# A list of steps for the first three slots, and weight loads in other places and packets, in a kernel of attention and soft mixture of experts

## The chip, the cores and the metric

The kernel runs on one core of one Trainium2 chip. The time is device microseconds of one execution; the figure for a kernel is the median of several runs. A profiled execution has its own time and, inside it, a span from the first to the last instruction; all positions below (such as "at 20.98") are microseconds from the start of that span. Engines are named as in the profile: PE is the matrix engine (PEld its weight loads), DVE the vector engine, ACT the scalar engine, POOL the general engine that also issues most DMAs, SP the engine that issues the rest.

## The reference

Attention first, with a softmax that has one extra term in its denominator, over 8 batches of 12 heads, 448 tokens and 64 features:

```python
scores = (q @ k.T) / sqrt(64)
m = max(scores); e = exp(scores - m)
attn = e / (sum(e) + exp(-m) + 1e-9)
x = (attn @ v)              # to [3584, 768], heads side by side
```

Then a soft mixture of 8 experts with 4 slots each. Logits `x @ phi` give two softmaxes: `d` over all 3584 rows, which mixes rows into 32 slots, and `c` over the 32 slots, which mixes the slots' results back.

```python
slot_input = d.T @ x                                   # [8, 4, 768]
slot_out[e] = relu(slot_input[e] @ w1[e]) @ w2[e]      # w1 768x1024, w2 1024x768
out = c @ slot_out                                     # [3584, 768]
```

q, k, v are 11 MB each in float32, w1 and w2 25 MB each; every one of them is turned to bfloat16 by the DMA that loads it. The row maximum must be known before the exponential is taken.

## The kernel before, in words

**Pairs and slots.** Two heads of one batch make a pair: 48 pairs, numbered n. The first part of the kernel is a loop over slots s = 0 to 48, each with two halves y = 0, 1; a slot handles one pair's attention and, beside it, earlier work of later pairs and later work of earlier ones. The engines' orders are written out by hand: an engine runs its instructions in the order in which the program issues them, so the place of a step in the loop is its place in every engine's queue.

**The steps of a pair n**, with the lines that the profile shows for them:

- `T(n)`: 28 transpositions of q and k pieces on PE (L255) into one bank, one copy out (L262 on ACT, for the first nine pairs always).
- `A(n, i)`, i in the order 0, 3, 1, 2: scores for the row maxima, two matmuls (L293, or L303 for i = 3) into banks of `psA`, which has three, and a maximum by DVE of each bank (L297, L306). `As(c)` takes the next c entries of the list `runs` of all (n, i). From slot 3 on most of them are fused into `Bk` (L284, L286).
- `W1(g)`: on POOL, the maxima of a group of pairs, negated and set out (L313, L317). `W2(g)`: four matmuls turn them (L335, L336). `W3(g)`: copy and exponentials on ACT (L341 to L347). Groups are pair 0; pairs 1 and 2; then three pairs each.
- `Bk(n, i)`: scores transposed (L366 or L395), the maximum taken off by a second matmul (L369 or L398), exponential on ACT (L371 or L401). Between the two matmuls it can issue one `A`.
- `AV(n, i, qs)`: products with V (L435), into the one bank of `psV`; `N1(n)` copies them out (L448, on ACT), `N2(n)` divides (two small DVE steps, then POOL, L468 to L479), `PX(n)` transposes the result (L500, copy L506).
- `V(g)`: POOL copies of v into its padded form (L407 to L410); `load(g, nm)` the DMAs of q, k or v for three pairs (L175, L179, L180, POOL).

After pair group b of six, the pieces `P(b)` of the logits and slot sums are hung into later slots (`post`).

**Weights.** `halves` lists w1 of the 8 experts (0 to 7), then w2 of the 8 experts (8 to 15), each a tile of 768 x 1024 bfloat16. Tiles 0 to 10 have memory of their own and are loaded in two transfers each during the loop: `half_at` says after which slot. w1 is read with rows p, p+128, ... on partition p, so that a packet is one row, 2,048 bytes in bfloat16; w2 with 8 neighbouring rows on a partition, so that half a tile is one packet of 6,144 bytes for each partition. Tiles 11 to 15 go, row by row (40 rows of 128 x 768), where the attention's own buffers lie, as these come free: `rows_at`. Some of the rows, `stage_at`, are first copied to a scratch tensor in HBM in bfloat16 (L145, POOL) and fetched from there late (L153, SP).

**End.** After slot 48: `hidden(g)` (w1 products of four experts, L848), `turn(g)` (transposes the hidden layer, L860; its columns are taken with a step of 8, to fit the 8 neighbouring rows of w2 on a partition), `slots(g)` (w2 products, L867), then the output (L904 to L926).

**The first slots.** Ahead of the loop the program issues, written out, T and A steps of pairs 0 to 2, the first group's `W1` to `W3`, and four DMAs; slots 0 to 2 then go through the loop with conditions of their own (`early`, `hs == 1`, `hs < 5`).

Of the kernel before, what the change touches and what calls it, by code (L numbers as in the profile page):

```python
# [9 lines left out]
BF16 = mybir.dt.bfloat16  # L10
# [21 lines left out]
def kernel(  # L32
# [10 lines left out]
    nc = tc.nc  # L43
    B, H, S, D = q.shape
    DD = H * D
# [63 lines left out]

    def load_part(i, z0, z1):  # L110
        kind, e = halves[i]
        src = (moe_w1 if kind == "w1" else moe_w2)[e].rearrange("(j p) f -> p j f" if kind == "w1" else "(p j) f -> p j f", p=128)
        gdma(out=w_sb[(kind, e)][:, z0:z1, :], in_=src[:, z0:z1, :])  # L113

    def load_half(i, z, t=None):
# [25 lines left out]
    def stage_rows(r0, r1):  # L141
        i, z = divmod(r0, FK)
        assert r1 <= (i + 1) * FK
        t = dram.tile([128, r1 - r0, DD], BF16, name=f"stage{r0}")
        gdma(out=t, in_=moe_w2[11 + i - E].rearrange("(p j) f -> p j f", p=128)[:, z:z + r1 - r0, :])  # L145
        staged[r0, r1] = t

# [8 lines left out]
    with ExitStack() as at:  # L156
# [83 lines left out]
        def T(n):  # L240
            g, pl = divmod(n, NP)
            first = n < NP * NP
            ps = psB.tile([128, 2, S], BF16, tag="b", name="ps_t")

            k0 = [psB.tile([128, 2, S], BF16, tag="b", name="ps_k") for _ in range(2)] if n == 0 else None
            for a in range(2):
                src = nat["qk"[a], g]
                order = [(tok, hl) for tok in range(7) for hl in range(2)]
                if a and n == 0:
                    order.sort(key=lambda z: kcol(z[1], z[0]))  # L250
                for tok, hl in order:
# [3 lines left out]
                    nc.tensor.transpose(o, src[r, pl, tok * D:(tok + 1) * D], ident[r, r])  # L255
# [428 lines left out]
        def As(c):  # L684
            for _ in range(min(c, len(runs))):
                A(*runs.pop(0))
# [3 lines left out]
        ps = psV.tile([128, 512], F32, tag="v", name="ps_idle")  # L690
        for _ in range(22):
            nc.tensor.matmul(ps[:, 0:64], wm[0][:, 0, :], wm[0][:, 0, 0:64], start=True, stop=True)
        T(0)
        As(2)
        T(1)
        As(2)
        W1(0)
        V(0)
        load(1, "v")
        ones_in(vp[1], nc.gpsimd)  # L700
        As(1)
        T(2)
        W2(0)
        W3(0)
        As(1)
        for nm in "qk":
            load(2, nm)
        for z in range(2):
            load_half(0, z, w_tile(0))

        half_at = {s: i + 1 for i, s in enumerate((1, 4, 7, 10, 13, 19, 22, 28, 31, 34))}


        rows_at = {77: 3, 83: 7, 85: 12, 89: 17, 91: 20, 92: 24, 93: 26, 95: 27}
        rows = 0
        stage_at = {18: (16, 24), 37: (27, 32), 38: (32, 36), 40: (36, 40)}
        wait_loads = []
        waits = [r for z in stage_at.values() for r in range(*z)]  # L720
        for s in range(NPAIR + 1):
            for y in range(2):
                hs = 2 * s + y
                early = int(hs < 4)
                mix = s >= 3 and len(runs) > 1 and runs[0][1] == 1 - y
                if mix:
                    Bk(s, 2 * y, mix=True)
                    Bk(s, 2 * y + 1, y, mix=True)
                else:
                    As(1)  # L730
                if mix:
                    pass
                elif s < NPAIR:
                    Bk(s, 2 * y)
                    As(early)
# [5 lines left out]
                if hs == 1:  # L741
                    W1(1)
                if hs < 5:
                    T(hs + 3)
                if y == 0:
                    if 0 <= s - 1:
                        for i in (2, 3):
                            AV(s - 1, i, range(3))
                else:
                    if 2 <= s < NPAIR - 6:  # L750
# [23 lines left out]
                As(early)  # L774
                if hs == 1:
                    W2(1)
                    W3(1)
                if y == 0 and s and s + 1 in firsts:
                    W1(mg(s + 1))
                if y == 0 and wait_loads:  # L780
                    f, z = wait_loads.pop()
                    f(z)
                if y == 0 and s % 3 == 2 and (s + 1) // 3 < NG:
                    if s == 2:
                        load(2, "v")
                    if s == NPAIR - 4:
                        V(NG - 1)
                    if s - 1 in half_at:
                        load_half(half_at[s - 1], 0, w_tile(half_at[s - 1]))
                if y == 0 and hs in rows_at:  # L790
                    load_rows(rows, rows_at[hs])
                    rows = rows_at[hs]
            def slot_loads(s):
                g = (s + 10) // 3
                if s == 1 or (s and s % 3 == 2):
                    if g < NG:
                        load(g, "q")
                        load(g, "k")
                g = (s + 9) // 3
                if s % 3 == 0 and g - 2 < NG - 1:  # L800
                    V(g - 2)
                    if s and g - 1 < NG:
                        load(g - 1, "v")
                if s - 1 in half_at:
                    load_half(half_at[s - 1], 1)
                if s in stage_at:
                    stage_rows(*stage_at[s])
# [47 lines left out]
        def turn(g):  # L855
            n = FK // (1 + g)
            for k0 in range(0, FK, n):
                ps = psA.tile([128, n, 128], BF16, tag="a", name="ps_ht")
                for kt in range(k0, k0 + n):
                    nc.tensor.transpose(ps[:, kt - k0, :], h[g].rearrange("p (d k) -> p k d", k=FK)[:, kt, :], ident)  # L860
# [156 lines left out]
```

## Time and profile before

| what | us |
|---|---|
| median of 3 runs (lowest, highest) | 300.39 (299.71, 301.83) |
| profiled execution | 300.82 |
| its span | 299.0 |
| last copy of attention products, L448 on DVE | 248.6 |
| busy PE, DVE, ACT, POOL in the span | 272.7, 249.7, 250.7, 193.3 |
| mean granted PE clock | 0.957 |

The 1.8 us between span and time lie around the instructions. A busy share is a mean over very different parts: a start of 34 us, in which the engines fill one after another; some 210 us in which PE, DVE and ACT are all nearly full; and the end, experts and output, in which they take turns. A "chain" line follows the work back from the last instruction; a "waits" line says which engine's line waited for whom. PE counts as busy while a matmul sits in it, even if that is slowed by another.

### The profile page before, as it was taken

To read this page: it belongs to the slowest core of one execution; us is meant where nothing else is said; L and a number is where in the kernel's file an instruction comes from. 1 tells how busy PE (TensorE), PEld (TensorE's weight loads), DVE (VectorE), ACT (ScalarE), POOL (GpSimd) and SP (SyncE) were. 2 spreads that over 40 slices of the span, in tenths; PEclk is the share of its full clock that TensorE was granted. 3 is DMA by queue.
4 is the path that set the end of the run, shared out by engine and by line. 5 is a ranking of instruction groups with operands and counts; after the bars stand their busy time and mean duration, and the time that the engine had idled before them with its cause. 6 is when DMAs were issued, how large, how long until landed. Compare 5 with 4: busy or idle time off the path is not lost.

```text
span 299.0 us, 12393 instructions
## 1 busy us (share of the span) xinstructions
PE 272.7 (91%) x5174; PEld 162.8 (54%) x5174; DVE 249.7 (83%) x581; ACT 250.7 (84%) x559; POOL 193.3 (65%) x389
## 2 busy tenths in 40 slices
PE   5989999999999999899999999999999999996810
PEld 4434556565666566557566666666565556652100
DVE  5889799999999999899999999998999675437930
ACT  4567999999899989898999899989999987337820
POOL 8791997879778959886969697978775633000000
PEclk9999999999999999999999999999999999997555
DMA  7999799999999978999998999999999689808997
GB/s 137 142 145 208 115 207 207 209 207 207 193 189 171 197 101 120 193 189 207 210 153 113 151 192 162 194 178 207 181 196 197 120 177 266 329 4 323 380 448 322
DMA packets 40103, 58.67 MB, mean 196 GB/s; under 512 B 2752, under 2 KB 30912, under 8 KB 39744
## 3 DMA queue, kind: packets, MB, share of 16 engines
q0 software_dynamic: 35072, 42.29, 85.8%
q1 hardware_dynamic: 4976, 15.60, 13.3%
q8 instruction: 40, 0.66, 0.8%
q14 instruction: 15, 0.12, 0.1%
HBM read 89.16 MB, written 15.14 MB: 349 GB/s over the span
## 4 chain that ended last, share of the span: by engine, by line
PE 73%; ACT 11%; DVE 5%; issue 3%; POOL 2%; DMA 1%; DVEq 0%; POOLq 0%; ACTq 0%
PE ps_av L435 16%; PE ps_a L284 11%; PE ps_b L366 8%; PE ps_b L369 7%; PE ps_t L255 6%; PE ps_b L395 5%; PE ps_b L398 3%; PE ps_x L500 3%; PE ps_o L910 3%; ACT W L401 2%; ACT W L262 2%; DVE mx L297 2%; ACT W L506 2%; PE ps_s L622 2%; PE ps_h L848 2%
## 5 line engine op out<-in xcount | busy, mean ns | idle before, releaser
L286 DVE TENSOR_REDUCE mx<-ps_a 128x1 f32<-128x448 f32 x250 | 137.4, 613 | 5.2 <-PE ps_a L284 4.4
L371 ACT ACTIVATE W<-ps_b 128x448 bf16<-128x448 f32 x250 | 120.4, 575 | 0.0
L284 PE MATMUL ps_a<-W 64*128 64x448 bf16 x250 | 80.8, 352 | 0.1
L366 PE MATMUL ps_b<-W 64*128 64x448 bf16 x250 | 70.2, 352 | 1.3
L369 PE MATMUL ps_b<-mT,sel 64*128 64x448 bf16 x250 | 66.3, 350 | 0.1
L435 PEld LDWEIGHTS <-W 128*128 128x128 bf16 (+1 forms) x1536 | 50.3, 100 | 27.4 <-issue 23.6
L435 PE MATMUL ps_av<-W 128*128 128x65 bf16 (+1 forms) x1536 | 64.5, 196 | 0.3 <-issue 0.3
L468 POOL TENSOR_TENSOR W<-ubuf,rec 128x384 bf16<-128x384 f32 x44 | 36.3, 826 | 38.6 <-ACT W L506 19.2
L401 ACT ACTIVATE W<-ps_b 128x448 bf16<-128x448 f32 x86 | 45.5, 572 | 4.2 <-PE ps_b L398 4.2
L255 PEld LDWEIGHTS <-W 64*64 64x64 bf16 x1344 | 29.2, 112 | 13.0 <-issue 4.7
L506 ACT CAST W<-ps_x 128x512 bf16<-128x512 f32 x47 | 28.6, 607 | 6.4 <-PE ps_x L500 6.1
L255 PE MATMUL ps_t<-ident,W 64*64 64x64 bf16 x1330 | 30.4, 195 | 2.6 <-ACT W L214 1.3
L306 DVE TENSOR_REDUCE mx<-ps_a 128x1 f32<-128x448 f32 x48 | 29.5, 615 | 1.5 <-PE ps_a L303 1.5
L284 PEld LDWEIGHTS <-W 64*128 64x128 bf16 x250 | 23.3, 94 | 9.8
L369 PEld LDWEIGHTS <-sel 64*128 64x128 bf16 x250 | 19.5, 94 | 14.8 <-issue 6.0
L395 PE MATMUL ps_b<-W 64*64 64x448 bf16 (+1 forms) x134 | 26.9, 374 | 0.3
L113 POOL DMA_DIRECT2D W<-in_moe_w_dram x30 | 20.9, 698 | 7.7 <-PE ps_b L398 7.7
L262 ACT COPY W<-ps_t 128x896 bf16<-128x896 bf16 x21 | 19.6, 933 | 7.2 <-PE ps_t L255 7.2
L448 ACT COPY ubuf<-ps_av 128x455 f32<-128x455 f32 x44 | 25.1, 571 | 0.3
L398 PE MATMUL ps_b<-mT,sel 64*64 64x448 bf16 (+1 forms) x134 | 24.9, 354 | 0.2
L297 DVE TENSOR_REDUCE mx<-ps_a 128x1 f32<-128x448 f32 x38 | 20.9, 616 | 2.1 <-PE ps_a L293 2.1
L479 POOL TENSOR_TENSOR W<-ubuf,rec 128x128 bf16<-128x128 f32 x44 | 17.6, 400 | 3.7
(156 smaller groups left out, 447.2 us busy)
## 6 DMA issues: line engine op xcount, KB each, us to landing
W<-in_moe_w_dram POOLq DMA_DIRECT2D x24, 768.0 KB, 10.1
W<-in_v_dram POOLq DMA_DIRECT2D x32, 192.0 KB, 6.4
out_dram<-W SPq DMA_DIRECT2D x2, 2688.0 KB, 10.0
W<-in_q_dram POOLq DMA_DIRECT2D x15, 336.0 KB, 6.2
W<-in_k_dram POOLq DMA_DIRECT2D x15, 336.0 KB, 7.2
out_dram<-W SPq DMA_DIRECT2D x6, 384.0 KB, 3.0
out_dram<-W SPq DMA_DIRECT2D x3, 768.0 KB, 4.9
W<-stage SPq DMA_DIRECT2D x3, 576.0 KB, 5.6
```

The lines of the kernel that those rows point to most:

```text
L255: nc.tensor.transpose(o, src[r, pl, tok * D:(tok + 1) * D], ident[r, r])
L284: nc.tensor.matmul(ps[:, 0:S], t[r, 0, i * 128:(i + 1) * 128], t[r, 1, :], start=True, stop=True)
L286: nc.vector.reduce_max(m[:, c:c + 1], ps[:, 0:S], axis=AX.X)
L366: nc.tensor.matmul(pss[hl][:, 0:S], t[rs[hl], 1, cols], t[rs[hl], 0, :], start=True, stop=False)
L369: nc.tensor.matmul(pss[hl][:, 0:S], sel[rs[hl], 2 * pl + hl:2 * pl + hl + 1].to_broadcast([64, 128]), mT[mg(n)][rs[hl], :], start=False, s ...
L371: nc.scalar.activation(e[:, hl, :], pss[hl][:, 0:S], AF.Exp, scale=scale)
L395: nc.tensor.matmul(outs[hl], t[rs[hl], 1, cols], t[rs[hl], 0, :], start=True, stop=False)
L398: nc.tensor.matmul(outs[hl], sel[rs[hl], 2 * pl + hl:2 * pl + hl + 1].to_broadcast([64, m]), mT[mg(n)][rs[hl], :], start=False, stop=True)
L401: nc.scalar.activation(e, p[:, 0:S], AF.Exp, scale=scale)
L435: nc.tensor.matmul(o, eT[n, i, hl][:, qc], vp[g % 2][:, 2 * pl + hl, i, 0:W65], start=(i == 0 and u == 0 and hl == 0) or (u == 3 and i == ...
L468: eng.tensor_mul(x[:, 0:3, c:c + 128].rearrange("p i (h d) -> p i h d", h=2), u[:, 0:6, 0:D].rearrange("p (i h) d -> p i h d", h=2), rec[: ...
L506: nc.scalar.copy(xT(b, pb), pss[0])
```

## The change

1. The w2 tiles of experts 0 to 3 are read as w1 is, row p, p+128, ... on partition p: packets of 1,536 bytes instead of 4,608 or 6,144. `turn(0)` accordingly takes 128 neighbouring columns instead of every eighth.
2. The scratch tensor gets rows that are 32 elements longer than their content, so that neighbouring rows no longer join: the staging and the fetches go in packets of 1,536 bytes.
3. `half_at` is every third slot from 4 to 31 instead of (1, 4, 7, 10, 13, 19, 22, 28, 31, 34). Rows 16 to 24 are staged in slots 35 and 36 instead of 18, rows 27 to 40 half a slot to two and a half slots later than before, each staging in two transfers. The second transfer of a tile is issued in the first half of the next slot, not at the end of its own.
4. Slots 0 to 2 and what stood ahead of them are one list of words, run in order. The steps and their number are the same, and so is the state at slot 3 (26 `A` steps taken, T up to pair 8); the tile 1 of w1 is no longer loaded in it. Between steps, the places differ: T(2) stands ahead of A(1,0) (before: between A(1,0) and A(1,3)); A(3,1) and A(3,2) ahead of `W2(1)` (before: behind it); products with V are cut into single steps i, with `A` or `Bk` between them.

```diff
-        src = (moe_w1 if kind == "w1" else moe_w2)[e].rearrange("(j p) f -> p j f" if kind == "w1" else "(p j) f -> p j f", p=128)
+        src = (moe_w1 if kind == "w1" else moe_w2)[e].rearrange(
+            "(j p) f -> p j f" if kind == "w1" or e < E // 2 else "(p j) f -> p j f", p=128)
...
-        t = dram.tile([128, r1 - r0, DD], BF16, name=f"stage{r0}")
+        t = dram.tile([128, r1 - r0, DD + 32], BF16, name=f"stage{r0}")[:, :, 0:DD]
...
-        T(0)
-        As(2)
-        T(1)
-        As(2)
-        W1(0)
-        V(0)
-        load(1, "v")
-        ones_in(vp[1], nc.gpsimd)
-        As(1)
-        T(2)
-        W2(0)
-        W3(0)
-        As(1)
-        for nm in "qk":
-            load(2, nm)
-        for z in range(2):
-            load_half(0, z, w_tile(0))
-        half_at = {s: i + 1 for i, s in enumerate((1, 4, 7, 10, 13, 19, 22, 28, 31, 34))}
+        half_at = {s: i + 1 for i, s in enumerate(range(4, 32, 3))}
...
-        stage_at = {18: (16, 24), 37: (27, 32), 38: (32, 36), 40: (36, 40)}
+        stage_at = {34: [(16, 20), (20, 24)], 37: [(27, 29), (29, 32)], 40: [(32, 36), (36, 40)]}
...
+        ramp = ("T0 A A T1 A A W0 T2 A G0 A X0 J0 A B0.0 A B0.1 A A T3 A B0.2 A A T4 C0.3 V0.0 W1 A V0.1 V0.2 A X1 T5 "
+                "A B1.0 A K0 V0.3 H0 C1.1 N0 B1.2 A T6 C1.3 V1.0 V1.1 A B2.0 M0 K1 A T7 B2.1 A V1.2 V1.3 W2 T8 H1 A "
+                "N1 B2.2 Y2 V2.0 X2 C2.3 Z0 V2.1 M1 K2 ")
+        for word in ramp.split():
...
+        for s in range(3, NPAIR + 1):
...
+                if y == 0 and s - 1 in stage_at:
+                    stage_rows(*stage_at[s - 1][0])
+                if y == 0 and s - 2 in half_at:
+                    load_half(half_at[s - 2], 1)
+                if y == 0 and s - 2 in stage_at:
+                    stage_rows(*stage_at[s - 2][1])
...
-                    nc.tensor.transpose(ps[:, kt - k0, :], h[g].rearrange("p (d k) -> p k d", k=FK)[:, kt, :], ident)
+                    nc.tensor.transpose(ps[:, kt - k0, :], h[g].rearrange("p (d k) -> p k d" if g else "p (k d) -> p k d", k=FK)[:, kt, :],
+                                    ident)
```

In the list, B and C are `Bk` (C with an `A` between its two matmuls), V one step i of `AV` for the first three blocks of rows and H the last block for all i, W is `W1`, X is `W2` with `W3`, N and M are `N1` and `N2`, Z is `PX(0)`. G is `V(0)`, the load of v for group 1 and its padding; J loads q and k of group 2 and tile 0 of w1; K(s) is what the end of slot s issued (K0: `V(1)`; K1: q and k of group 3; K2: of group 4); Y loads v of group 2.

More of the change, by code (lines that the diff above doesn't have):

```diff
@@ L716, with slot_loads @@
         rows_at = {77: 3, 83: 7, 85: 12, 89: 17, 91: 20, 92: 24, 93: 26, 95: 27}
         rows = 0
-        stage_at = {18: (16, 24), 37: (27, 32), 38: (32, 36), 40: (36, 40)}
+        stage_at = {34: [(16, 20), (20, 24)], 37: [(27, 29), (29, 32)], 40: [(32, 36), (36, 40)]}
         wait_loads = []
-        waits = [r for z in stage_at.values() for r in range(*z)]
-        for s in range(NPAIR + 1):
+        waits = [r for z in stage_at.values() for y in z for r in range(*y)]
+        def slot_loads(s):
+            g = (s + 10) // 3
+            if s == 1 or (s and s % 3 == 2):
+                if g < NG:
+                    load(g, "q")
+                    load(g, "k")
+            g = (s + 9) // 3
+            if s % 3 == 0 and g - 2 < NG - 1:
+                V(g - 2)
+                if s and g - 1 < NG:
+                    load(g - 1, "v")
@@ new lines @@
+        ramp = ("T0 A A T1 A A W0 T2 A G0 A X0 J0 A B0.0 A B0.1 A A T3 A B0.2 A A T4 C0.3 V0.0 W1 A V0.1 V0.2 A X1 T5 "
+                "A B1.0 A K0 V0.3 H0 C1.1 N0 B1.2 A T6 C1.3 V1.0 V1.1 A B2.0 M0 K1 A T7 B2.1 A V1.2 V1.3 W2 T8 H1 A "
+                "N1 B2.2 Y2 V2.0 X2 C2.3 Z0 V2.1 M1 K2 ")
+        for word in ramp.split():
+            op, arg = word[0], [int(z) for z in word[1:].split(".") if z]
+            if op == "T":
+                T(*arg)
+            elif op == "A":
+                As(1)
+            elif op in "BC":
+                Bk(*arg, int(op == "C"))
+            elif op == "W":
+                W1(*arg)
+            elif op == "X":
+                W2(*arg)
+                W3(*arg)
+            elif op == "V":
+                AV(*arg, range(3))
+            elif op == "H":
+                for i in range(4):
+                    AV(arg[0], i, [3])
+            elif op == "N":
+                N1(*arg)
+            elif op == "M":
+                N2(*arg)
+            elif op == "G":
+                V(0)
+                load(1, "v")
+                ones_in(vp[1], nc.gpsimd)
+            elif op == "J":
+                for nm in "qk":
+                    load(2, nm)
+                for z in range(2):
+                    load_half(0, z, w_tile(0))
+            elif op == "Y":
+                load(2, "v")
+                if 1 in half_at:
+                    load_half(half_at[1], 0, w_tile(half_at[1]))
+            elif op == "Z":
+                PX(0)
+            elif op == "K":
+                slot_loads(*arg)
@@ L722 @@
+        for s in range(3, NPAIR + 1):
             for y in range(2):
                 hs = 2 * s + y
-                early = int(hs < 4)
-                mix = s >= 3 and len(runs) > 1 and runs[0][1] == 1 - y
+                mix = len(runs) > 1 and runs[0][1] == 1 - y
                 if mix:
@@ L734 @@
                     Bk(s, 2 * y)
-                    As(early)
                     side = int(y == 1 and len(runs) > 0 and runs[0][1] == 3)
@@ L740 @@
                     As(1)
[L741 to L744, printed above, removed]
                 if y == 0:
-                    if 0 <= s - 1:
-                        for i in (2, 3):
-                            AV(s - 1, i, range(3))
+                    for i in (2, 3):
+                        AV(s - 1, i, range(3))
                 else:
-                    if 2 <= s < NPAIR - 6:
+                    if s < NPAIR - 6:
                         T(s + 6)
@@ L773 @@
                         N2(s - 1)
[L774 to L777, printed above, removed]
                 if y == 0 and s and s + 1 in firsts:
@@ L783 @@
                 if y == 0 and s % 3 == 2 and (s + 1) // 3 < NG:
-                    if s == 2:
-                        load(2, "v")
                     if s == NPAIR - 4:
@@ L792 @@
                     rows = rows_at[hs]
[L793 to L807, printed above, removed]
             if s > 2 and s + 2 in firsts:
```

## The prediction

> **What bounds the kernel now.** First the page's busy times and its 40 slices (7.5 us each).
>
> ```profile
> PE 272.7 (91%) x5174; PEld 162.8 (54%) x5174; DVE 249.7 (83%) x581; ACT 250.7 (84%) x559; POOL 193.3 (65%) x389
> PE   5989999999999999899999999999999999996810
> DVE  5889799999999999899999999998999675437930
> ACT  4567999999899989898999899989999987337820
> ```
>
> From slice 5 to 31 PE, DVE and ACT are all at 8 or 9: a stretch with nothing to gain from moving a step, except where a slice dips. The first four slices are lower, ACT's most. One slice inside dips on all three rows (slice 17, from 120 us). So I asked for the engines' sums in the start and just behind it (columns: length, then busy PE, PEld, DVE, ACT, POOL, granted clock, DMA share, GB/s).
>
> ```profile
> 5.70:34.10 28.40, 25.93 (x415) 13.31 (x414) 25.08 (x49) 18.85 (x37) 18.79 (x44) 1.00 1.00 147
> 34.10:41.90 7.80, 7.42 (x124) 3.94 (x124) 6.49 (x13) 7.80 (x20) 7.47 (x13) 1.00 1.25 205
> ```
>
> From the first maximum to slot 3 DVE works 25.08 of 28.40 us: it is the engine nearest to full, and 3.32 us are idle. Behind it ACT is busy 7.80 of 7.80: the start leaves a backlog there, and the chain of work runs on ACT from 33.16 to 40.5. A gain in the start counts only if ACT, too, gets its work earlier. The places where DVE idled (the bracket: us idle, and who ended it):
>
> ```profile
> 11.97 0.62 DVE L306 TENSOR_REDUCE mx<-ps_a 128x1 f32<-128x448 f32 x1 [0.92 <-PE ps_a L303]
> ...
> 20.98 3.28 DVE L297 TENSOR_REDUCE mx<-ps_a 128x1 f32<-128x448 f32 x6 [0.67 <-PE ps_a L293]
> 24.70 0.62 DVE L306 TENSOR_REDUCE mx<-ps_a 128x1 f32<-128x448 f32 x1 [0.43 <-PE ps_a L303]
> ...
> 31.92 1.16 DVE L297 TENSOR_REDUCE mx<-ps_a 128x1 f32<-128x448 f32 x2 [0.48 <-PE ps_a L293]
> ```
>
> Each time PE was on something else (T, W2, V products) and the three banks of `psA` had run dry. Two smaller gaps, 0.36 at 7.78 and 0.18 at 19.70, and the delays between instructions make the rest.
>
> The dip in slice 17 is on PE's own timeline:
>
> ```profile
> 124.37 0.44 PE L255 MATMUL ps_t<-ident,W 64*64 64x64 bf16 x17
> 125.69 0.35 PE L255 MATMUL ps_t<-ident,W 64*64 64x64 bf16 x11 [0.87 <-issue]
> ...
> 214.05 0.28 PE L435 MATMUL ps_av<-W 128*128 128x65 bf16 x4 [0.35 <-issue]
> ```
>
> PE stops between the 17th and 18th of 28 transpositions, with no semaphore to wait for ("issue"), and again inside four V products at 213.7. These are the only two such stops of over 0.2 us in the full stretch. What they share is in the DMA view of the first one's stretch, 119 to 127:
>
> ```profile
> DMA packets 299, 1.72 MB, mean 215 GB/s; under 512 B 16, under 2 KB 249, under 8 KB 249
> q0 software_dynamic: 297, 1.69, 109.3%
> q8 instruction: 1, 0.02, 0.8%
> ```
>
> 50 packets are over 8 KB: 48 of them are the staging of rows 16 to 24, 1,536 KB, so 32 KB each; the trace's packet records give them 2.43 to 3.43 us apiece. The q8 packet is one of 40 in the run, 16 KB each, with PE's instructions. On average one comes every 250 PE instructions; this one, at 123.46, comes 410 behind the last. I read it as a refill that sat behind 32 KB packets until PE ran out. At 211.36 the next such packet takes 1.39 us (others 0.9 to 1.0) among packets of 7,680 bytes (587 ns), and PE stops at 213.71. No refill beside packets of 2,048 (173 ns) or 6,144 bytes (474 ns) is followed by a stop.
>
> **The change part by part.**
>
> *The list of steps.* All 26 A keep their order and number, so DVE has the same 25 us of work; only gaps can go. T(2), 0.96 us of PE, now stands ahead of A(1,0): A(1,0) starts later, A(1,3) right behind it; of 0.92 I count 0.45 gone. At 20.98 PE waited for `W1(1)`, which POOL reached at 19.76 behind five us of DMAs and memsets; that POOL order is unchanged, but A(3,1) and A(3,2) now stand ahead of `W2(1)`, four maxima of 0.55 (3.28 for six), so DVE works through: 0.67 and 0.18 gone. At 24.70, T(5) and 20 V products (0.72) lay between two A; now A(4,0) parts them: 0.43 gone. At 31.92, twelve V products (0.47), T(8) (0.56) and H1 lie between A(5,2) and A(6,0): stays. Sum 0.45 + 0.67 + 0.18 + 0.43 = 1.73.
>
> ACT the same way: from `W3(1)` at 20.69 to slot 3's first exponential at 35.47 it has 14 exponentials, 4 copies of T, 2 of N1, and 1.7 of the rest. Back to back (29.36 to 35.47) an exponential takes 0.43, a T copy 0.79, an N1 copy 0.43: 6.0 + 3.2 + 0.9 + 1.7 = 11.8. Against 14.8 that is 3.0 at most. Putting the new order down with these durations, three A banks, and DVE without the gaps above, slot 3's exponential starts near 33.7: 1.7 gained. Both agree on **1.7**.
>
> What is late next: q and k of group 3. Here k landed at 37.30 and T(9) starts to load at 37.82. Their issue (31.02) stands behind `N2(0)` on POOL, and `N2(0)`'s two DVE steps now stand behind one maximum more (0.55), which eats most of DVE's lead there; so k lands some 0.5 earlier, T(9) would like 1.7 earlier, and PE waits about 0.7. ACT is the full engine there and has three exponentials queued; I count 0.2. **Net 1.5.** Bounds: 0 (ACT's backlog takes the gaps) and 3.0.
>
> *Packets and places.* No packet over 8 KB from POOL is left in the full stretch, and none of 7,680 bytes. The two stops are 0.87 + 0.35 = 1.22. By the N1 copies, which come once a slot, six slots take 29.03 (70.50 to 99.53) and 28.98 (158.73 to 187.71), but 29.96 (99.53 to 129.49) and 29.51 (187.71 to 217.22): 0.95 + 0.50 = 1.45. I take **1.4**; bounds 0 (the stops recur elsewhere) and 1.7.
>
> What it costs: a 1,536-byte packet takes 134 ns, four of them 536 against 474 for one of 6,144: 13% more DMA time for w2 of four experts and for the staging. A group of three slots then needs 1,024 x 134 + 768 x 88 + 768 x 60 ns over 16 engines = 15.7 us of packet time for w2, q, k and v, against 15.4 with a w1 tile, in 14.5 us; packets overlap, the share reached 1.23 with w1, and no T waited. So nothing is added: the cover is 3.5 slots between a load of q and k and its T. If that went, a T would wait. POOL issues with three pieces for each partition take 0.78 against 0.58; some 0.2 to 0.3 x 10 on an engine that is idle for a third. Bound: 1.0 lost.
>
> *turn(0).* Its loads of the matrix engine step by 8 elements; the others of 128 x 128 do not:
>
> ```profile
> L860 PEld LDWEIGHTS <-ubuf x8: 142/148/166, 260.5 to 261.0; 128*128 128x128 bf16 x8
> ```
>
> Against a median of 97 for L500's. Eight loads by 50 ns are 0.4, partly under the transpositions: I take **0.1**, bounds 0 and 0.4. By the Trainium skill, "TensorE: Matmul & The Clock Gate", section "Weight-path perf modes", the fast load holds for any column step up to 1,024 elements, so the step would cost nothing and this term be 0; the row, 148 against 97, speaks against it.
>
> *Sum.* 1.5 + 1.4 + 0.1 = 3.0. The profiled execution took 300.82 (span 299.0 and 1.8 around it), so 297.8; it lies 0.4 above the median of the runs shown, so the forecast for that is **297.4**.
>
> **Rivals.** *(a) Only the packets count:* ACT's full stretch behind slot 3 and the wait of T(9) take the start's gain. For it: 7.80 of 7.80, and 0.5 us of slack at T(9). Against: ACT idled 2.3 us between 21.4 and 29.4. 300.4 - 1.5 = 298.9. *(b) The change doesn't do what it says:* the stops come from the refill's own timing, not from long packets, and show up elsewhere; the start gains a little: 300.0. For it: only two cases. Against: some 25 refills beside packets of 512 to 6,144 bytes without a stop. *(c) Slower: late w2.* The stagings of rows 32 to 40 move from 211.6 and 222.4 to about 222 and 227, where rows 3 to 12 are loaded too. Eight rows of 128 packets of 134 ns over 16 engines are 8.6 us of DMA time, in a stretch whose share was 1.08 (220 to 230) and 0.65 (230 to 240). The last fetch landed at 262.03, and the w2 products of experts 4 to 7 that need it start near 266: the margin is 4 us. If all 8.6 us are late, PE waits 4.4: 297.4 + 4.4 = 301.8. It decides from a delay of 4 us on; beyond +1% it leads only from 10 us on. Against: 3.5 us of free DMA time from 230 to 240. The Trainium skill, "DMA: Bandwidth & Descriptors", section "Rules for kernel authors", wants transfers coalesced, 1 MiB and more, which speaks for (c); no row here shows a PE wait from short packets. *(d) More:* DVE's gaps all go and ACT follows (3.0), and 1.7 for the packets: 295.6.
>
> **How the numbers follow.** A measurement of this kernel tells about 1% (3 us) from no change; the forecast lies on that bound. Chances: forecast 0.55 (half of it beyond the bound), (a) 0.17, (b) 0.08, (c) 0.12 (half of it with a delay of over 10 us), (d) 0.08. Faster: 0.28 + 0.08, and 0.07 from (a), should the packets alone bring twice what I count: 0.43. Slower: 0.06. Same: the rest, 0.51. The range, 295.4 to 300.8, leaves out the outer ends of (c) and (d).
>
> **What would show it.** Right: no PE stop by "issue" over 0.2 us between 34 and 245; q8 packets evenly spaced; DVE idle under 1.8 us up to slot 3; slot 3's first exponential near 33.7; T(9) with a short wait for q or k. Wrong: a PE wait for DMA behind 255; slot 3 no earlier; a stop by "issue" at some other place; ACT as full behind slot 3 and its first exponential at 35.

## The result, and the profile after

| | before | after |
|---|---|---|
| median (lowest, highest), 20 runs each | 300.45 (299.29, 307.34) | 298.47 (297.57, 300.78) |
| ratio of after to before, 95% | | 0.993 (0.991 to 0.9949) |
| profiled execution, its span | 300.82, 299.0 | 300.78, 299.0 |

The change gains 0.7%, 1.98 us by the medians; 297.4 was forecast for the median and 295.4 to 300.8 as the range. Before's 307.34 is one of the few runs that are slow as a whole, and the ratios leave such runs out. The profiled execution of after is the longest of its 20 runs, so its trace shows losses that the typical run has less of. A second profile of the same kernel (e3, below) took 298.90.

First the page's busy times and slices of the profile after:

```profile
PE 271.4 (91%) x5174; PEld 162.5 (54%) x5174; DVE 249.7 (84%) x581; ACT 249.8 (84%) x559; POOL 195.9 (66%) x391
PE   5999899999999999999899999999999999996820
DVE  5899799999999989999889999998999675537930
ACT  3569999999899989998989899989999987337820
```

The work is the same, but the dips have moved: PE's slice 17 (from 120 us) is 9 now, and slice 20 (from 142 us) is 8. The sums of the start and of what follows it (length, then busy PE, PEld, DVE, ACT, POOL, granted clock, DMA share, GB/s):

```profile
5.70:34.10 28.40, 26.09 (x424) 13.65 (x423) 25.50 (x50) 20.04 (x42) 19.61 (x45) 1.00 1.04 157
34.10:41.90 7.80, 7.66 (x160) 4.54 (x158) 7.31 (x16) 7.80 (x18) 6.51 (x13) 1.00 1.22 181
```

ACT did 1.19 us more in the same 28.40 (it had 18.85), and still is busy 7.80 of 7.80 behind it. The best marker for the rest of this text is the copy `N1` of each slot's attention products (`ubuf` from `ps_av`, L449 now), once a slot at fixed places of the work. Each entry is its start after minus its start before:

| copy of slot | 5 | 10 | 15 | 20 | 25 | 30 | 45 | whole execution |
|---|---|---|---|---|---|---|---|---|
| after | -1.62 | -1.61 | -1.61 | -0.96 | -1.63 | +0.10 | +0.12 | -0.04 |
| after once more (e3) | -1.61 | -1.61 | -1.61 | -0.92 | -2.15 | -2.20 | -1.94 | -1.92 |

The start gains 1.6 us, and keeps it up to slot 16. Then both executions lose 0.65 to 0.69 at one place. Between slots 20 and 25 before itself loses 1.2, around its stop at 124.8, and e3 is 2.15 ahead; the profiled execution of after loses 2.3 between slots 20 and 30. The waits that answer to this, on the timeline of after (start, length, engine, line, tiles, and in the bracket the idle time ahead and who ended it), DVE first:

```profile
10.52 1.16 DVE L298 TENSOR_REDUCE mx<-ps_a 128x1 f32<-128x448 f32 x2 [0.40 <-PE ps_a L294]
...
30.22 1.16 DVE L298 TENSOR_REDUCE mx<-ps_a 128x1 f32<-128x448 f32 x2 [0.48 <-PE ps_a L294]
32.75 0.62 DVE L307 TENSOR_REDUCE mx<-ps_a 128x1 f32<-128x448 f32 x1 [1.37 <-PE ps_a L304]
```

Of the gaps shown of before, 0.92 has become 0.40, those of 0.67 and 0.43 are gone, that of 0.48 stands as it was. A new one of 1.37 is ahead of the list's last maximum. PE's timeline of after:

```profile
31.11 0.34 PE L436 MATMUL ps_av<-W 128*128 128x65 bf16 x6 [0.62 <-ACT ubuf L449]
32.01 0.34 PE L336 MATMUL ps_m<-ident,W 128*128 128x128 bf16 x3 [0.55 <-POOL W L314]
104.06 0.34 PE L336 MATMUL ps_m<-ident,W 128*128 128x128 bf16 x3 [0.59 <-POOL W L314]
143.26 0.38 PE L256 MATMUL ps_t<-ident,W 64*64 64x64 bf16 x12 [0.60 <-issue]
150.01 0.52 PE L436 MATMUL ps_av<-W 128*128 128x65 bf16 x12 [1.10 <-issue]
164.05 0.35 PE L256 MATMUL ps_t<-ident,W 64*64 64x64 bf16 x11 [0.34 <-issue]
201.96 0.22 PE L436 MATMUL ps_av<-W 128*64 128x65 bf16 x2 [0.48 <-issue]
```

The first two are what PE waited for inside DVE's 1.37: V2.0 waits for N1(1), and `W2(2)` waits for `W1(2)` on POOL. The third is the loss of 0.6 near slot 17, again a wait for POOL. The last four, 2.52 us, are stops of the kind that the shorter packets were forecast to end: they name no semaphore, and there is no packet over 2,048 bytes from POOL near them.

### The profile page after: what moved, and what is told of

Same layout as the page of the kernel before. It is cut to its first block, busy times and chain, and to the rows that moved or that the text cites. A ratio compares the mean times of both kernels' runs of the same rounds, so it can differ in the third digit from the quotient of the medians.

```text
span 299.0 us, 12398 instructions
## 1 busy us (share of the span) xinstructions
PE 271.4 (91%) x5174; PEld 162.5 (54%) x5174; DVE 249.7 (84%) x581; ACT 249.8 (84%) x559; POOL 195.9 (66%) x391
## 4 chain that ended last, share of the span: by engine, by line
PE 68%; ACT 10%; DVE 6%; POOL 6%; issue 4%; DMA 2%; DVEq 0%; POOLq 0%; ACTq 0%
PE ps_av L436 15%; PE ps_a L285 10%; PE ps_b L367 7%; PE ps_b L370 7%; PE ps_t L256 5%; PE ps_b L396 5%; PE ps_x L501 3%; PE ps_b L399 3%; ACT W L402 2%; PE ps_o L925 2%; DVE mx L298 2%; PE ps_s L623 2%; PE ps_h L862 2%; PE ps_so L882 2%; ACT W L263 2%
## 5 line engine op out<-in xcount | busy, mean ns | idle before, releaser
L114 POOL DMA_DIRECT2D W<-in_moe_w_dram x30 | 22.6, 755 | 7.9 <-PE ps_b L399 7.8
L449 ACT COPY ubuf<-ps_av 128x455 f32<-128x455 f32 x44 | 25.1, 571 | 0.8 <-POOL W L408 0.6
```

## The experiments

All compare with the kernel before on the same chip: e1 to e4 on one (before's median there was 301.4), e7 to e10 on a second (300.81), e5, e6, e12 and e13 on a third (301.64). Across these sets ratios are to be compared, not times. "Over lowest" is how far a kernel's median lies above its own lowest run. "Profiled" is the time of the execution that the profile shows: a profile of a kernel's fastest run says little of the losses of its usual one.

| run | list of steps | places | packets | median (runs) | ratio to before (95%) | over lowest | profiled |
|---|---|---|---|---|---|---|---|
| e1 | new | old | long | 299.34 (12) | 0.9925 (0.9893 to 0.9956) | 1.6 | 297.78 |
| e2 | old | new | short | 300.07 (12) | 0.9975 (0.9948 to 1.0001) | 0.7 | 300.76 |
| e3 (= after) | new | new | short | 298.66 (12) | 0.9914 (0.988 to 0.9948) | 0.6 | 298.90 |
| e4 | new | fewer loads | short | 298.05 (6) | 0.9899 (0.9864 to 0.9935) | 0.2 | 299.42 |
| e5 | old | new | long | 301.78 (12) | 1.0019 (0.9994 to 1.0044) | 2.0 | 304.73 |
| e6 | old | old | short | 300.47 (12) | 0.9967 (0.9942 to 0.9993) | 1.2 | 300.29 |
| e7 | new | new | long, w1 too | 298.97 (12) | 0.9951 (0.9926 to 0.9976) | 1.0 | 297.98 |
| e8 | reordered | new | short | 297.73 (6) | 0.9902 (0.9871 to 0.9932) | 0.6 | 297.88 |
| e9 | new | moved | short | 298.03 (12) | 0.9912 (0.9883 to 0.9942) | 0.6 | 298.24 |
| e10 | reordered | moved | short | 297.67 (6) | 0.9903 (0.9871 to 0.9934) | 0.6 | 297.97 |
| e12 | reordered | moved | long | 297.32 (6) | 0.9885 (0.9843 to 0.9927) | 0.8 | 297.61 |
| e13 (= e10) | reordered | moved | short | 297.27 (6) | 0.9876 (0.9844 to 0.9907) | 0.6 | 297.77 |

"Short" has turn(0)'s new reading with it. The kernel before lay 1.9, 1.6 and 2.4 over its lowest run in the three sets. The profile of e5 was taken in an execution 2.9 us over its median and is not read for stops.

### e1, e2, e3: the two halves of the change apart

e1 is after with these lines of before:

```diff
-            "(j p) f -> p j f" if kind == "w1" or e < E // 2 else "(p j) f -> p j f", p=128)
+            "(j p) f -> p j f" if kind == "w1" else "(p j) f -> p j f", p=128)
-        t = dram.tile([128, r1 - r0, DD + 32], BF16, name=f"stage{r0}")[:, :, 0:DD]
+        t = dram.tile([128, r1 - r0, DD], BF16, name=f"stage{r0}")
-        half_at = {s: i + 1 for i, s in enumerate(range(4, 32, 3))}
+        half_at = {s: i + 1 for i, s in enumerate((1, 4, 7, 10, 13, 19, 22, 28, 31, 34))}
```

and with `stage_at`, the places of the second halves and turn(0) of before. e2 is the other half: the start of before, all else of after. e3 is after.

> Only the list of steps for the first three slots; weights, packets and turn(0) as before. Theory R (the list brings the gain, the packets and places nothing that lasts): the copies of the V products (one a slot) come 1.6 us earlier from slot 1 on, the median is 1.6 below the kernel before, and PE still has stops of 0.3 to 1.1 us with no releaser in the full stretch. Theory P (the forecast: list 1.5, packets 1.4): also 1.5 below before, but then 1.4 above the changed kernel in runs without an odd stop; the stop beside the 32 KB staging (slot 21) is there.

> The first three slots as before; packets, places of the weight loads and turn(0) as in the changed kernel. Theory R: within 0.5 us of the kernel before (0.1 from turn(0), 0 to 0.3 from the places), stops in the profile as many as before. Theory P: 1.4 below before, no stop over 0.2 us between 34 and 245.

> The changed kernel once more, for a second profile. Its first profile lay at 300.78, the highest of its 20 runs, with five stops of PE of together 3.1 us beside packets of 1,536 and 2,048 bytes. Theory R (stops come by chance, whatever the packets): median 298.5; stops again, at other places, together 0.5 to 2 us. Theory P (that profile was an exception): no stop over 0.2 us.

The list alone puts N1 1.59 us ahead by slot 16. With the rest alone N1 is 0.15 ahead, but from its first copy on, so that is a difference between the profiled starts. Together it is 1.61. So the start's gain belongs to the list.

The times say the same of the two halves. By the ratios the list alone gains 2.3 us (more than the 1.5 to 1.6 of either theory), the rest alone 0.75, with an interval that reaches zero. On top of the new start the rest adds 0.3 by the ratios of e1 and e3, 0.7 by their medians. That is less than the intervals can tell from nothing, and less than the 1.5 that was forecast for it. The wait of PE for POOL (0.58 at 104.94 in e2, 0.57 at 103.48 in e3) comes with the new places or packets; e1 doesn't have it. The profiles of e2 and e3 have one stop by "issue" each without any packet over 2,048 bytes from POOL beside it (0.76 at 200.72, 0.72 at 199.18). That is against the prediction's reading of the stops. The profile of e1 has none over 0.3 us between 34 and 250 although the 32 KB packets are in it; but it shows the fastest of e1's 12 runs, and the median lies 1.6 us above that, so its other runs may well have had stops.

### e4: fewer loads

```diff
+    for i in range(1, 10):
+        w_view(i, w_tile(10))
-        half_at = {s: i + 1 for i, s in enumerate(range(4, 32, 3))}
+        half_at = {4: 10}
```

Tiles 1 to 9 (w1 of experts 1 to 7, w2 of experts 0 and 1) are not loaded; the products that use them read w2 of expert 2 instead.

> The changed kernel without the loads of w1 of experts 1 to 7 and of w2 of experts 0 and 1: these products read the tile of w2 of expert 2 instead, so the arithmetic and all instructions of PE, DVE and ACT are the same, the DMA queue of the loop is empty for half of the time. If PE's stops are instruction refills that queue behind loads, of whatever packet length: no stop over 0.2 us in the full stretch, every instruction packet begins within 300 instructions of its due place, and the median is 0.8 to 1.5 below the changed kernel. If a refill is late for a reason of its own: stops as in the changed kernel and the same time.

No stop by "issue" was left in the stretch, though the profile is of the slowest of the six runs, and the median lies 0.2 over the lowest. It is 0.6 below e3's, not the 0.8 to 1.5 that were expected. How late a refill is can be counted: the trace has 40 packets of 16 KB on the instruction queue (q8) and 10,356 PE instructions, so one packet for about 256; the count is of PE instructions started when packet k starts, less 256 k, with k from 0. In e4, between 34 and 255 us, the ten refills that start with no load in flight come at 195 to 234; those with loads in flight at 234 to 371. The same ten refills in e3, where loads are in flight, come at 187 to 342, and eight of them at 284 or more. So **loads make refills late**. (In e4 T(9) waits 1.11 us for k, a wait that no other kernel here has; its time is therefore not compared closely.)

### e5, e6: places and packets apart, with the old start

e5 is before with `half_at`, `stage_at` and the middle-of-slot places of after; e6 is before with the packets, the padding and turn(0).

```diff
 e5
-        half_at = {s: i + 1 for i, s in enumerate((1, 4, 7, 10, 13, 19, 22, 28, 31, 34))}
+        half_at = {s: i + 1 for i, s in enumerate(range(4, 32, 3))}
 e6
-            "(j p) f -> p j f" if kind == "w1" else "(p j) f -> p j f", p=128)
+            "(j p) f -> p j f" if kind == "w1" or e < E // 2 else "(p j) f -> p j f", p=128)
```

> The kernel before with the changed places of the loads alone (halves at slots 4 to 31, the second of each at the middle of its slot, staging in pieces at 34, 37 and 40); packets, padding, turn(0) and start as before. What is asked is how far the median lies over the kernel's own lowest run, since a run without stops is the lowest: with the packets and places of before that was 1.6 to 1.9 us (kernel before, e1), with those of the changed kernel .6 to .9. Theory of the prediction (long packets make the stops): 1.2 to 2.0, median 300.7 to 301.4. Rival (the places do, since a refill then finds fewer loads ahead of it): .5 to .9, median 299.9 to 300.4. In both, POOL's stop at 16,384 packets falls on the q load near 94 and TensorE waits .57 near 105, so the lowest run is no lower than that of before, 299.2 to 299.9.

> The kernel before with the packets alone (w2 of experts 0 to 3 as 2,048 bytes, staging padded to 1,536, turn(0) by the new reading); places and start as before. Theory of the prediction: median .5 to .9 over the lowest, lowest 299.0 to 299.4 (turn .1), median 299.7 to 300.2. Rival (places, not packets): 1.2 to 2.0 over the lowest, median 300.5 to 301.2. No wait of TensorE near 104 in either, since POOL's stop falls on the second v load near 87.

The places alone gain nothing (1.0019), and e5's 2.0 over the lowest run is what the prediction's theory expected of long packets. The packets alone gain 0.33% (1.0 us, interval 0.2 to 1.7); their 1.2 over the lowest is the foot of the rival's range, not the theory's 0.5 to 0.9. So with the old start the packets seem to help, though not by ending all stops. e5 against e2 (1.0019 against 0.9975, 1.3 us) points the same way, but these are two chips and the intervals overlap. Yet e6's profile still has a stop by "issue" of 0.77 at 200.6 beside packets of 1,536 bytes, and a wait of another kind at 148.78: `W2` waits 0.7 us for POOL, whose copies of v stood waiting for a load (the timeline of POOL in e6, columns as above):

```profile
143.71 0.66 POOL L408 COPY W<-W 128x576 bf16<-128x576 bf16 x1 [1.74 <-DMA W<-in_v_dram]
```

### e7: long packets everywhere, with the new start and places

```diff
-        src = (moe_w1 if kind == "w1" else moe_w2)[e].rearrange(
-            "(j p) f -> p j f" if kind == "w1" or e < E // 2 else "(p j) f -> p j f", p=128)
+        src = (moe_w1 if kind == "w1" else moe_w2)[e].rearrange("(p j) f -> p j f", p=128)
```

and no padding, turn(0) as before.

> The changed kernel with every weight tile loaded in long packets (6,144 and 3,072 bytes instead of 2,048 and 1,536), no padding of the staging copy and turn(0) by its old reading. Its first expert products use the rows of w1 in another order, so its numbers are of other products; the work is the same in kind and amount. Theory of the prediction (a refill of TensorE's instructions stops it when it stands behind long packets): the .5 to 1.4 us of stops come back, at 2 to 4 places, and turn(0) costs .1: lowest time as the changed kernel's, 297.6, median 299.0 to 300.0. Rival (a refill stops TensorE when it starts late behind loads of any length): as many and as long stops as the changed kernel in its two profiles (.7 to 2.5 us in all), median within .4 of it, 298.3 to 299.0. A further reading rides on it: with 128 packets in place of 384 for each half, the loads pass 16,384 packets at the k load near 107 us and not at the q load near 93; if that count is what makes POOL stop for .75 us at 93, the stop moves to 107, and TensorE's wait of .57 us for POOL near 103.5 is gone (N1 from slot 17 on 1.6 us ahead of before, not 1.0).

298.97 lies where the ranges of the theory and of the rival meet, and decides nothing. By the ratios e7 is 1.1 us above e3, and on its own chip 0.9 above e9; but the intervals overlap, and its profile, with no stop by "issue" over 0.3, is of its fastest run. Its N1 falls 0.35 behind between slots 5 and 10: there PE has a stop of 0.21 by "issue" at 66.79, 2.2 us behind a refill with a count of 342 beside packets of 6,144 bytes. The rider on it came out: POOL stops ahead of the k load at 107.8 and no longer at 93, and PE's wait near 103.5 is gone (N1 -1.13 at slots 10, 15 and 20 alike). The line of POOL in e7:

```profile
108.43 0.78 POOL L175 DMA_DIRECT2D W<-in_k_dram  x1 [0.64 <-PE ps_b L398]
```

### e8: the end of the list in another order

```diff
-  "A B1.0 A K0 V0.3 H0 C1.1 N0 B1.2 A T6 C1.3 V1.0 V1.1 A B2.0 M0 K1 A T7 B2.1 A V1.2 V1.3 W2 T8 H1 A "
-  "N1 B2.2 Y2 V2.0 X2 C2.3 Z0 V2.1 M1 K2 "
+  "A B1.0 A K0 V0.3 H0 C1.1 N0 K1 B1.2 A T6 C1.3 V1.0 V1.1 A B2.0 M0 A T7 B2.1 A W2 V1.2 V1.3 H1 A N1 T8 "
+  "B2.2 Y2 X2 C2.3 V2.0 Z0 V2.1 M1 K2 "
```

> The changed kernel with another order of the last two lines of the list of steps: the q and k loads of group 3 ahead of M0, W2 ahead of V1.2, H1 and N1 ahead of T8, X2 and C2.3 ahead of V2.0. Theory: the 1.37 us gap of DVE at 31.4 and TensorE's waits of .59 and .55 at 30.5 and 31.5 come from this order (W2 waits for W1(2), which stands on POOL behind those two loads): they shrink to under .3 each, slot 3's first exponential comes .5 to 1.0 earlier (33.0 to 33.5 instead of 33.95), N1 of slots 4 to 16 is 2.1 to 2.6 us ahead of before instead of 1.6, and the median falls by .5 to 1.0, to 297.5 to 298.0. Rival (the start is set by ScalarE's work, and the waits only move): the same waits elsewhere, N1 as in the changed kernel within .2, median 298.2 to 298.9.

PE's two waits of 0.6 are gone (the longest left in the stretch is 0.21 for ACT), DVE's gap is 0.77 instead of 1.37:

```profile
31.90 0.62 DVE L307 TENSOR_REDUCE mx<-ps_a 128x1 f32<-128x448 f32 x1 [0.77 <-PE ps_a L304]
```

The first N1 is 0.3 later than in after (the profiled starts differ by that much), and from it to N1 of slot 5 it takes 24.38 against 24.91: 0.53 gained, the lower end of what was expected. Measured from the start of the span, N1 is 1.84 ahead of before, not 2.1 to 2.6, slot 3's first exponential comes at 33.70, not 33.0 to 33.5, and DVE's gap did not fall under 0.3. The median, 297.73, is where the theory had it. e8 keeps the wait near 103.5 (0.62).

### e9: two loads moved ahead of the point where POOL stops

In after, POOL stands still before a q load, and this is what PE's wait at 103.5 goes back to: POOL has no idle time between 93 and 103 to make up for it. The timeline of POOL in after:

```profile
92.30 0.40 POOL L480 TENSOR_TENSOR W<-ubuf,rec 128x128 bf16<-128x128 f32 x1
93.45 0.83 POOL L176 DMA_DIRECT2D W<-in_q_dram  x1 [0.75 <-PE ps_b L370]
94.28 0.77 POOL L176 DMA_DIRECT2D W<-in_k_dram  x1
95.07 0.54 POOL L591 TENSOR_TENSOR z<-lb,lb 128x160 f32<-128x160 f32 x1
95.54 0.78 POOL L114 DMA_DIRECT2D W<-in_moe_w_dram  x1
96.35 0.84 POOL L469 TENSOR_TENSOR W<-ubuf,rec 128x384 bf16<-128x384 f32 x1
```

The bracket names PE, but the semaphores that this load waits for had been reached long before. Counting what POOL's loads issue (one packet for each run of bytes, and 16 closing ones of 4 bytes for each load, as the packet records have them), 16,160 packets are issued ahead of this load and 16,560 with it. The idea behind e9 is that POOL stops at some count in between; the 16,384 of the expectation is a guess at it. e9 moves two halves to the front of this load:

```diff
-        half_at = {s: i + 1 for i, s in enumerate(range(4, 32, 3))}
+        half_at = {s: i + 1 for i, s in enumerate((1, 4, 7, 10, 13, 19, 22, 25, 28, 31))}
```

> The changed kernel with tiles 1 to 5 loaded three slots earlier (halves at slots 1, 4, 7, 10, 13 instead of 4, 7, 10, 13, 16; the others as they are), which moves two halves ahead of the q load near 93 us. Theory (POOL stops for .6 to .75 us ahead of the load with which the packets issued so far would pass 16,384): it stops ahead of the second v load near 85.5, where .75 us of POOL's own idle time at 91 takes it up; TensorE's wait of .57 at 103.5 is gone, N1 stays 1.5 to 1.7 us ahead of before up to slot 30, and the median falls by .4 to .6, to 297.9 to 298.1. Rival (the stop belongs to this q load or to a place in POOL's program): the stop stays at 92.7 to 93.5 or moves by two instructions only, the wait at 103.5 stays, median as the changed kernel's, 298.3 to 298.8.

The timeline of POOL in e9:

```profile
84.73 0.73 POOL L180 DMA_DIRECT2D W<-in_v_dram  x1
86.10 0.67 POOL L181 DMA_DIRECT2D W<-in_v_dram  x1 [0.63 <-issue]
...
91.14 0.83 POOL L469 TENSOR_TENSOR W<-ubuf,rec 128x384 bf16<-128x384 f32 x1 [0.83 <-ACT W L507]
...
92.66 0.82 POOL L176 DMA_DIRECT2D W<-in_q_dram  x1
```

The stop is where it was expected, ahead of the second v load, and POOL's idle time at 91, 0.83 now, takes it up; the q load starts at 92.66 with no gap. PE's wait near 103.5 is gone and N1 of slot 20 is 1.59 ahead (after 0.96). Behind slot 20 this execution loses 0.7 to a break of PE of 0.62 at 147.73, 2 us behind a refill with a count of 365. The median, 298.03, is in the range expected; by the ratio (0.9912) it can't be told from e3's 0.9914, for 0.57 us is less than the intervals.

### e10 and e13: both

> The order of e8 and the places of e9 together. If both theories hold, the gains add: N1 2.1 to 2.6 us ahead of before throughout, no wait of TensorE over .3 us outside the start but refill stops, median 297.0 to 297.6, lowest 296.4 to 297.0. If only the second holds: 297.9 to 298.1; if only the first: 297.5 to 298.0; if neither: 298.3 to 298.8. The earlier half in the start adds .77 us of POOL's time behind the load of v at 33 us; if that is late for POOL's next work there, the start loses up to .4 of its gain.

> e10 once more, beside e12 on the same chip: the list of e8, the places of e9, the packets of the changed kernel. Median 297.4 to 297.9, ratio to before .988 to .993; TensorE's waits of .6 at 30.5, 31.5 and 103.5 absent, N1 of slot 5 some 24.4 us behind the first N1 (before 26.6, changed kernel 24.9).

From the first N1 to slot 5 it takes 24.38 us in both; no wait for POOL over 0.3 is left. e10's median is 297.67, just above the 297.0 to 297.6 expected if both gains add, and 0.06 below e8's on the same chip; e13's is 297.27, just below its range. Their ratios, 0.9903 and 0.9876, are 0.1 and 0.4% below e3's 0.9914, with intervals that overlap. So the trace shows both waits gone, but the times do not show that the second gain adds to the first. In e10 the first N1 was 0.76 later than before and in e13 0.26; it is the same kernel, so this differs from one execution to the next. e13's profile has one stop by "issue" (0.63 at 103.98).

### e12: e10 with long packets

```diff
-            "(j p) f -> p j f" if kind == "w1" or e < E // 2 else "(p j) f -> p j f", p=128)
+            "(j p) f -> p j f" if kind == "w1" else "(p j) f -> p j f", p=128)
```

and no padding, turn(0) as before.

> The list of e8 and the places of e9 with the packets of the kernel before (w2 as 6,144 bytes, staging as 32 KB, no padding, old reading in turn(0)). Theory of the prediction (length of packets makes the stops): median 1.0 to 1.6 over the lowest, 298.3 to 299.0 against 297.5 to 297.9 with short packets. Rival (length does not matter): median 297.6 to 298.0, which is turn(0)'s .1 over e13; stops in the profile of the same number and size.

Nearer the rival: 297.32 against 297.27, 0.8 over the lowest against 0.6. Its profile, of a usual run, has no stop by "issue" over 0.3, though three refills with counts of 364, 375 and 389 stood beside packets of 6,144 bytes. With this order the length of the packets is worth nothing that six runs can tell.

### All profiles together

In the 13 profiles without e5's, 442 refills start between 34 and 255 us. None of the 394 that come at a count under 344 is followed by a stop by "issue" of over 0.3 us; 3 of 27 between 344 and 359 are, and 8 of 21 at 360 or more, among them all five at 398 or more. (One of the 8 is e9's 0.62 at 147.73, which the profile puts to an earlier line of PE itself, done when the break began.) Of the 48 late refills, at 344 or more, 13 ran beside a packet of 6,144 bytes or more and 2 of these are followed by a stop; 35 ran beside shorter ones and 9 are. A profile of a kernel with long packets (before, e1, e7, e12) has 4 or 5 late refills, of one with short packets 2 to 5 (e4, with fewer loads, has 1). The profile of e5, left out, has four stops of 0.41 to 0.74, behind refills at 344 to 420 beside packets of 6,144 bytes.

So in these profiles a stop goes with a late refill, and not with long packets beside it. Two things keep this from being the whole answer. Most late refills have no stop behind them. And the profiles are single executions: e1's and e7's are of their fastest run, after's, with four of the stops, of its slowest. The medians lie 0.8 to 2.4 us over the lowest run in the kernels with long packets and 0.2 to 1.2 in those with short ones, so that long packets cost something in other executions is not ruled out.

## Why the prediction was right, and where it was wrong

**The list of steps (1.5 net): right in size.** N1 gained 1.62, 1.59 with the list alone. DVE's gaps went as counted (0.92 to 0.40, 0.67 and 0.43 gone, 0.48 kept), and slot 3's first exponential starts at 33.95 (33.7 forecast, 35.47 before). Two details failed. T(9) loads with no wait (0.2 was taken off for it), because its loads are issued 1.2 us earlier, at 29.81. And "what is late next" was another consumer of the same two loads: `W1(2)` stands behind them on POOL, so `W2(2)` waits and DVE idles 1.37 us; up to slot 3 it idled 2.90 in all (28.40 - 25.50), where the sign was under 1.8. e8, which moves these loads and some steps around them, wins 0.53. So the sum came out near the measured gain partly by luck: DVE's idle time in the window fell by 0.42, not by 1.73, and the new gap and the missing wait of T(9) pull in opposite ways.

**Packets and places (1.4): the step that failed.** It read the stops as refills behind packets of 32 KB and 7,680 bytes and argued that none beside 2,048 bytes is followed by a stop. After's own profile has four, up to 1.10 us, beside 2,048 and 1,536 bytes, and e2, e3, e6 and e13 have one each. By the prediction's own list a stop at some other place was a sign of being wrong. For this term rival (b) was nearer: stops recur elsewhere, behind late refills; what (b) had too low was the start's gain. Two stops in one profile were too few to tell length from lateness: the refills ahead of them came at 400 and 346 by the count, and another at 378, beside 6,144 bytes, had no stop. In e1 a refill beside the same 32 KB packets, at 120.43 with a count of 347, had none either.

With turn(0)'s 0.1 in it and the wait for POOL below against it, this half of the change brought 0.3 (e1 to e3) to 0.75 us (e2) by the ratios, where 1.5 was forecast. What the packets are worth alone depends on what they stand with: some 1.0 (e6) with the old start, nothing that can be told with e13's order. Why they pay with one and not with the other stays open. That loads in flight make refills late is shown (e4); which loads make one late is not.

**A cost at nothing that was not nothing.** The prediction put POOL's side of the new places at a few tenths on an idle engine. The new order of loads moved POOL's stop from the second v load (0.62 at 87.1 before, taken up by idle time) to the q load in front of a full stretch of POOL's work, and PE loses 0.57 to 0.62 there in each kernel with these places and w1 in packets of 2,048 bytes (after, e2, e3, e5, e8). By subtraction, 1.98 - 1.62 + 0.57 - 0.1 = 0.8 is left for packets and places in the median of after; that is a remainder, not a measurement.

**turn(0) (0.1): right.** Its weight loads, by the view of that line in after:

```profile
L874 PEld LDWEIGHTS <-ubuf x8: 96/98/99, 260.7 to 261.0; 128*128 128x128 bf16 x8
L874 PEld LDWEIGHTS <-W x8: 143/148/166, 263.4 to 263.8; 128*128 128x128 bf16 x8
```

98 ns without the step, 148 with it (group 1, unchanged), in one execution. On PE the eight transpositions of turn(0) take 0.71 us in before and 0.62 in after. The Trainium skill ("TensorE: Matmul & The Clock Gate", "Weight-path perf modes") keeps the fast load at such a step, from which the prediction weighed a cost of nothing: here the step of 8 elements costs 50 ns for each load, and the measurement decides.

**Rivals.** (c), late w2, didn't come: no PE wait for DMA behind 255, and from the last N1 to the end after takes 50.29 us, before 50.45. (Its sum had a slip: 8.6 less the margin of 4 is 4.6, not 4.4.) The rule of the Trainium skill that was cited for it ("DMA: Bandwidth & Descriptors", "Rules for kernel authors") is on the size of a whole transfer. A half of a weight tile stays one transfer of 768 KB here, and only its packets get shorter; these are some 1.0 us faster with the old start and level with long ones in e12 and e13, so they show no price. (a) had nearly the right number, 298.9, by a mechanism that did not happen: the start's 1.6 us were kept, not taken by ACT. (d) is out with the sizes above. The median missed the forecast by 1.07 us: 0.57 for POOL's stop and the rest, 0.5, in the term of packets and places. It lies in a range of 5.4 us, in which three of the four rivals lie as well, so that it lies there does not speak for the reading of the stops.

## What to carry to other kernels

Two events that share a neighbour are no cause: before naming one, count the same neighbour where nothing happened, and look for a quantity that separates the cases better (here how late a refill is, more than what lies beside it). See where a profiled execution lies among its kernel's runs before reading anything from what its profile lacks. When loads are moved, list what stands behind each on its issuing engine, at its old place and at its new one, that engine's own stops among them. One copy that comes once a slot, compared between two profiles, shows a gain or a loss as a step at its place.

## What the runs showed that was not expected

- **POOL stops once, for 0.61 to 0.98 us, ahead of the load with which its packets since the start pass some count between 16,160 and 16,416**, in all 14 profiles: 16,160 are issued before it in twelve, 16,144 in e7, 16,016 in e4, the next load having 400. 16,384, a power of two, lies in this range, but no run fixes the number. Which load it is follows from the order and the packets alone: the second v load at 85 to 88 us (before, e1, e6, e9, e10, e12, e13), the q load at 93 to 95 (after, e2, e3, e5, e8), at 109 in e4, the k load at 108 in e7. Before, e1, e4, e5, e7 and e12 stop a second time, for 0.5 to 1.0 us, some 13,200 to 14,000 packets later (before at 183.3); why at that number, and why others don't, is open.
- **Refills of PE's instructions are late by the loads in flight**: 195 to 234 instructions past their due count with none, 234 to 371 with some (e4); in the 13 profiles the stops of PE over 0.3 us, up to 1.10, are behind refills at 346 or more.
- Between slots 6 and 41 an undisturbed stretch of six slots takes 28.91 to 29.04 us in every profile but e5's, so most of what differs there between two executions is in single breaks.
